# Three first columns of q and k instead of two in fp32, with the expert weights in another buffer

## The chip, the cores and the metric

The kernel runs on one core of a Trainium2 chip. The metric is the device time of one execution in microseconds (us). Most runs of one kernel here lie within half a microsecond of its median, and single ones are a microsecond longer, so differences below that need many runs. All runs quoted are in the fast state; "a slow run" below means only one of the longer runs within it. Engines: PE is TensorE (PEld its weight loads), DVE VectorE, ACT ScalarE, POOL GpSimd, SP SyncE.

## The reference, cut to what matters

```python
# attention over channels: B, N, C = 4, 6400, 256
qn = q / (norm(q, axis=1) + 1e-06);  kn = k / (norm(k, axis=1) + 1e-06)
a = softmax(kn.transpose(0, 2, 1) @ qn / tau)        # 256 x 256 for each batch
x = (v @ a).reshape(B * N, C)
# two of 8 experts by gate, adapters of rank 16
out = x + sum_e w_e * (x @ A[e]) @ B[e]
```

For each batch all of q and k has to be read before the 256 x 256 matrix is complete; only then can v be used. Inputs and output are fp32 in HBM: 78.91 MB are read and 26.21 MB written.

## The kernel before: the parts that matter

A small planner in Python decides the order of instructions on each engine; at run time each engine keeps that order. q and k of a batch are cut into 50 columns of 128 rows x 256 values and loaded in three pieces, most of them by GpSimd with a cast to bf16 during the DMA. The first piece of batch 0 is special: it is cut into 2 + 15 columns, and the 2 columns come in fp32 from SyncE (q) and ScalarE (k), whose DMAs can be issued at time 0. ScalarE then casts them.

```python
PARTS = {(0, 0): ((0, 2), (2, 15)), ...}
# ... cut ...
def load_consts():
    first = W["first"].rearrange("p c d -> p (c d)")         # the same buffer "y0" as q and k below
    W["A0"] = first[0:P // 4, 4 * C:8 * C].rearrange("p (e g r) -> p e g r", e=E, r=R)
    nc.sync.dma_start(W["A0"], moe_A.rearrange("e (p g) r -> p e g r", g=8))
    W["B0"] = first[:, 8 * C:9 * C]
    nc.scalar.dma_start(W["B0"], moe_B.rearrange("e r d -> (e r) d"))
    W["wg0"] = first[0:P // 4, 9 * C:9 * C + 4 * CC * E].rearrange(...)
    nc.scalar.dma_start(W["wg0"], moe_w_gate.rearrange(...))
# ... cut ...
def do_load(s, what, b, i, c, n):
    # ... cut ...
        if (b, c) == (0, 0):
            if "first" not in W:
                W["first"] = sbuf.tile([P, PC, C], FP32, tag="y0", name="y")
            lo = "qk".index(what) * n
            W[what] = W["first"][:, lo:lo + n, :]
            early.append((nc.sync if what == "q" else nc.scalar).dma_start(W[what], src[b, :, 0:n, :]))
            return
    nc.gpsimd.dma_start(t[:, c - c0:c - c0 + n, :], src[b, :, c:c + n, :])
# ... cut ...
def do_cast(s, what):
    nc.scalar.copy(held["qk", (what, 0, 0), ""][:, 0:PARTS[0, 0][0][1], :], W[what])
```

`y0` and `y1` are output buffers, free until the first outputs are written after 60 us.

## Time and profile before

| | before |
|---|---|
| time, median of 3 runs | 255.24 us (255.18 to 255.48) |
| the profiled run | 256.1 us, span 254.3 us |
| TensorE busy | 85% |
| GpSimd's DMA queue, share of the 16 DMA engines | 74.9% |

The page's slices of the kernel before (40 equal slices of 6.4 us; a digit is the busy share in tenths; GB/s counts bytes written):

```profile
PE   1064993799999998999979999979999979999970
...
DMA  9999999999999999999999999999999999999994
GB/s 201 210 216 209 212 222 210 211 219 216 213 218 211 304 290 293 272 217 217 213 215 221 214 215 218 214 209 344 287 273 338 333 328 315 315 421 427 416 411 167
```

Its queue table (queue, packets, MB written, share of the 16 engines' span):

```profile
q0 software_dynamic: 7488, 39.06, 74.9%
q1 hardware_dynamic: 3968, 26.61, 25.7%
q10 hardware_dynamic: 336, 0.40, 0.5%
```

q0 is GpSimd's casting queue: it writes half of what it reads. 39.06 MB in 190 us (74.9% of the span) is 205 GB/s written, so about 410 GB/s read.

TensorE's waits up to 70 us in the kernel before (us in total, times, longest):

```profile
PE acc L571 <- DMA qk<-in_k_dram: 14.0, 3, 9.2
PE acc L571 <- ACT qk L751: 4.8, 1, 4.8
```

The same in the timeline (start, us, instruction, idle time before it and what ended it):

```profile
4.81 1.03 PE L571 MATMUL acc<-qk 128*128 128x256 bf16 x4 [4.81 <-ACT qk L751]
...
15.06 2.32 PE L571 MATMUL acc<-qk 128*128 128x256 bf16 x10 [9.21 <-DMA qk<-in_k_dram]
...
25.35 0.39 PE L571 MATMUL acc<-qk 128*128 128x256 bf16 x2 [3.47 <-DMA qk<-in_k_dram]
```

TensorE uses the two early columns by 5.8 us, then stands still until the 15-column k lands, then again until the 17-column k lands. And the chain of waits of the kernel before (start, us, what):

```profile
4.74 25.52 DMA qk<-in_k_dram
...
30.54 22.25 DMA v<-in_v_dram
```

Two DMA pieces make up 47.8 us of the first 52.8 us of the chain.

### The profile page before, as it was taken

What the parts mean: (1) busy time and instruction counts of PE and PEld (TensorE: products, weight loads), DVE (VectorE), ACT (ScalarE), POOL (GpSimd) and SP (SyncE); (2) the same over time, 40 slices, a digit from 0 to 9 for tenths busy, and PEclk for the clock granted to TensorE, in tenths of its full rate; (3) what the DMA queues carried; (4) which work ended last, traced back from release to release, by engine and by line L of the source; (5) the groups of instructions that cost most, each with busy time, mean ns of one, the idle gap of its engine ahead of it and who ended that gap; (6) DMA issues with size and microseconds to landing.
All of it is one profiled execution on the core that took longest, in us unless ns stands there. A gap on an engine that the chain in (4) does not pass through costs nothing.

```text
span 254.3 us, 6342 instructions
## 1 busy us (share of the span) xinstructions
PE 215.6 (85%) x2641; PEld 192.6 (76%) x2643; DVE 190.2 (75%) x486; ACT 167.2 (66%) x270; POOL 30.0 (12%) x58
## 2 busy tenths in 40 slices
PE   1064993799999998999979999979999979999970
PEld 0043891588999996799879999769999869999860
DVE  0045579779989987898979995689888888888910
ACT  4354447457787666888848768452867969768770
POOL 7000220040020002000030100510000210000000
PEclk9999799799999999999999999999999999999997
DMA  9999999999999999999999999999999999999994
GB/s 201 210 216 209 212 222 210 211 219 216 213 218 211 304 290 293 272 217 217 213 215 221 214 215 218 214 209 344 287 273 338 333 328 315 315 421 427 416 411 167
DMA packets 11820, 66.47 MB, mean 261 GB/s; under 512 B 1424, under 2 KB 2320, under 8 KB 7184
## 3 DMA queue, kind: packets, MB, share of 16 engines
q0 software_dynamic: 7488, 39.06, 74.9%
q1 hardware_dynamic: 3968, 26.61, 25.7%
q10 hardware_dynamic: 336, 0.40, 0.5%
q8 instruction: 20, 0.33, 0.5%
q14 instruction: 8, 0.07, 0.1%
HBM read 78.91 MB, written 26.21 MB: 413 GB/s over the span
## 4 chain that ended last, share of the span: by engine, by line
PE 49%; DMA 39%; ACT 3%; DVE 3%; POOL 2%; issue 1%; ACTq 0%; POOLq 0%
DMA qk<-in_k_dram 22%; PE Y_ps L890 13%; DMA v<-in_v_dram 9%; DMA qk<-in_q_dram 8%; PE acc L571 7%; PE Y_ps L894 6%; PE T_ps L766 6%; PE ZL_ps L788 4%; PE gzT_ps L877 3%; PE acc L580 2%; PE acc L575 2%; PE Z_ps L857 2%; DVE a_bf L740 2%; ACT a_exp L692 1%; PE log_ps L803 1%
## 5 line engine op out<-in xcount | busy, mean ns | idle before, releaser
L571 PE MATMUL acc<-qk 128*128 128x256 bf16 x400 | 71.0, 286 | 21.0 <-DMA qk<-in_k_dram 15.7
L599 DVE TENSOR_TENSOR ssq<-ssq,sq 128x1280 f32<-128x1280 f32 (+1 forms) x27 | 43.4, 1607 | 27.6 <-ACT sq L593 25.6
L890 PE MATMUL Y_ps<-a_bf,vT 128*128 128x256 bf16 x400 | 60.0, 273 | 0.0
L593 ACT ACTIVATE sq<-qk 128x1280 f32<-128x1280 bf16 (+1 forms) x27 | 36.9, 1366 | 26.5 <-DVE ssq L599 19.7
L746 ACT COPY y<-Y_ps 128x512 f32<-128x512 f32 x79 | 45.8, 587 | 12.3 <-PE Y_ps L894 9.8
L571 PEld LDWEIGHTS <-qk 128*128 128x128 bf16 x400 | 33.9, 103 | 25.0 <-DMA qk<-in_k_dram 17.4
L746 ACT COPY vT<-T_ps 128x1024 bf16<-128x1024 bf16 (+1 forms) x44 | 37.0, 871 | 6.7 <-PE T_ps L766 6.5
L890 PEld LDWEIGHTS <-vT 128*128 128x128 bf16 x400 | 37.6, 98 | 3.7
L894 PE MATMUL Y_ps<-ball,gzT 128*128 128x256 bf16 x200 | 38.2, 273 | 0.3 <-DVE gzT L748 0.3
L575 PE MATMUL acc<-qk 128*128 128x128 bf16 x242 | 34.4, 225 | 0.0
L556 POOL DMA_DIRECT2D v<-in_v_dram x20 | 12.2, 611 | 128.4 <-PE T_ps L766 80.8
L766 PE MATMUL T_ps<-ident,v 128*128 128x128 bf16 x400 | 26.9, 219 | 0.4 <-DMA v<-in_v_dram 0.4
L575 PEld LDWEIGHTS <-qk 128*128 128x128 bf16 x242 | 24.5, 101 | 3.6
L766 PEld LDWEIGHTS <-v 128*128 128x128 bf16 x400 | 23.8, 98 | 1.6 <-DMA v<-in_v_dram 1.2
L866 DVE TENSOR_TENSOR gz<-zl,gateg 128x512 bf16<-128x512 f32 (+1 forms) x42 | 23.5, 597 | 0.3
L580 PE MATMUL acc<-qk 128*128 128x128 bf16 x168 | 23.7, 224 | 0.0
L894 PEld LDWEIGHTS <-gzT 128*128 128x128 bf16 x200 | 19.4, 98 | 3.0 <-DVE gzT L748 0.6
L788 PE MATMUL ZL_ps<-waA_sb,vT 128*128 128x136 bf16 x280 | 19.6, 222 | 1.1 <-DVE waA_sb L734 0.9
L877 PE MATMUL gzT_ps<-ident,gz 128*128 128x128 bf16 x200 | 19.7, 219 | 0.3
L593 ACT ACTIVATE ssq<-qk 128x1536 f32<-128x1536 bf16 x8 | 11.9, 1483 | 11.1 <-DMA qk<-in_q_dram 6.2
L748 DVE COPY gzT<-gzT_ps 128x512 bf16<-128x512 bf16 (+1 forms) x39 | 15.0, 390 | 5.5 <-PE gzT_ps L877 4.8
L788 PEld LDWEIGHTS <-vT 128*128 128x128 bf16 x280 | 17.6, 98 | 1.8 <-issue 1.5
(79 smaller groups left out, 272.3 us busy)
## 6 DMA issues: line engine op xcount, KB each, us to landing
out_dram<-y SPq DMA_DIRECT2D x18, 1280.0 KB, 18.2
v<-in_v_dram POOLq DMA_DIRECT2D x20, 640.0 KB, 20.5
qk<-in_q_dram POOLq DMA_DIRECT2D x7, 1088.0 KB, 23.9
qk<-in_k_dram POOLq DMA_DIRECT2D x7, 1088.0 KB, 28.8
qk<-in_q_dram POOLq DMA_DIRECT2D x2, 1024.0 KB, 18.7
qk<-in_k_dram POOLq DMA_DIRECT2D x2, 1024.0 KB, 23.0
out_dram<-y SPq DMA_DIRECT2D x4, 512.0 KB, 7.0
qk<-in_q_dram POOLq DMA_DIRECT2D x2, 512.0 KB, 17.3
```

Of the source, the lines that this page charges most:

```text
L571: nc.tensor.matmul(acc[ic][:, 0:256], kt[:, j, ic * P:(ic + 1) * P], qt[:, j, :], start=c == 0, stop=False, skip_group_check=True)
L575: nc.tensor.matmul(acc[ic][:, 256:384], kt[:, j, ic * P:(ic + 1) * P], kt[:, j, ic * P:(ic + 1) * P], start=False, stop=False, skip_group_ ...
L580: nc.tensor.matmul(acc[ic][:, 384:512], qt[:, j, ic * P:(ic + 1) * P], qt[:, j, ic * P:(ic + 1) * P], start=False, stop=c == NC - 1, skip_ ...
L593: nc.scalar.activation(out[:, 0:n, :], t[:, j:j + n, :], ACT.Square)
L599: nc.vector.tensor_tensor(out=t, in0=t, in1=held["sq", (w, b, g), ""][:, 0:n, :], op=OP.add)
L746: nc.scalar.copy(out, in_)
L766: nc.tensor.matmul(ps[:, ic, j, :], vt[:, c + j, ic * P:(ic + 1) * P], W["ident"], is_transpose=True, start=(ic + j == 0), stop=(ic == CC ...
L788: nc.tensor.matmul(ps[:, j, :], vT[:, ic, c + j, :], st[b]["waA"][:, ic, :], start=(j == 0 and ic == 0), stop=(j == n - 1 and ic == CC - 1 ...
L866: nc.vector.tensor_tensor(out=gz.rearrange("p c (e r) -> p c e r", e=E), in0=z.rearrange("p c (e r) -> p c e r", e=E), in1=held["gate", (b ...
L877: nc.tensor.matmul(ps[:, j, :], gz[:, j, :], W["ident"], is_transpose=True, start=(j == 0), stop=(j == n - 1))
L890: nc.tensor.matmul(ps[:, j, :], vT[:, ic, c + j, :], st[b]["a"][:, ic, :], start=(j == 0 and ic == 0), stop=False, skip_group_check=True)
L894: nc.tensor.matmul(ps[:, j, :], gzT[:, c + j - UNITS[u][0], :], W["B"], start=False, stop=(j == 1), skip_group_check=True)
```

## The change

Its intent: SyncE's and ScalarE's queues start before GpSimd's, so let them bring one column more and let TensorE do it in its idle time. Three fp32 columns of q and k reach over the old place of A, so A, B and the gate weights move to the next buffer. The order of instructions stays the same on every engine.

```diff
+FIRST = 3
@@ load_consts
-        first = W["first"].rearrange("p c d -> p (c d)")
+        first = sbuf.tile([P, PC, C], FP32, tag="y1", name="y").rearrange("p c d -> p (c d)")
@@ do_load
             if (b, c) == (0, 0):
+                n = FIRST
                 if "first" not in W:
@@ do_load
                 return
+        if (what, b, i) in (("q", 0, 0), ("k", 0, 0)):
+            c, n = FIRST, c + n - FIRST
         nc.gpsimd.dma_start(t[:, c - c0:c - c0 + n, :], src[b, :, c:c + n, :])
@@ do_cast
-        nc.scalar.copy(held["qk", (what, 0, 0), ""][:, 0:PARTS[0, 0][0][1], :], W[what])
+        nc.scalar.copy(held["qk", (what, 0, 0), ""][:, 0:FIRST, :], W[what])
```

## The prediction

> What bounds the kernel now. The page's slices show the 16 DMA engines 9 tenths busy or more in 39 of 40, and the queue table says why: the casting GpSimd queue holds 74.9% of the engines' time, SyncE's queue (stores, q's first load) 25.7%. Both cost the same per fp32 byte: 39.06 MB written as bf16 in 190 us is 205 GB/s, so about 410 GB/s read; SyncE's 26.61 MB in 65 us is 407 GB/s. TensorE is second: 85% busy, near 10 tenths from 55 to 245 us. Before that it follows the loads: by the list of waits its accumulation waits 14.0 us for k to land (9.2 of it until 15.05 us, 3.5 until 25.35 us). The chain of waits is one DMA piece from 4.74 to 30.26 us and another (v) from 30.54 to 52.8 us.
>
> What the change does. No engine's order of instructions changes. q's and k's first fp32 loads grow from 256 to 384 KB each; the next GpSimd loads shrink from 15 to 14 columns. HBM bytes read stay equal; 0.13 MB more is written to SBUF. The casts grow from 0.61 us to an estimated 0.85 us each (from this trace's copies, 587 ns for 512 columns, 871 ns for 1024). The weights move to the second output buffer, since three columns reach over their old place; they are consumed by 37 us, and no output is written before 60 us, so this costs nothing.
>
> What lies on the critical path. Not TensorE's third column: it is 2 matmuls, about 0.5 us (4 took 1.03 us), moved from behind 15.05 us into idle time; but afterwards TensorE waits for the 17-column k load until 25.35 us anyway, so only that wait grows. What could count is the DMA: the first GpSimd load is issued at 1.42 us and its first packet appears about 3.6 us; until then only the fp32 loads and weights feed the engines. In narrow windows the engines move nothing from 4.5 to 4.6 us and little until 4.8. From 2 to 5 us they read (written bytes plus the GpSimd bytes once more) an estimated 1.10 MB of the 1.24 that about 410 GB/s would give, a loss near 0.35 us. 256 KB (0.64 us at 407 GB/s) moved to queues that start first can fill part of that hole. I credit 0.1 to 0.3 us, which shifts every later load, since the GpSimd queue hardly runs empty afterwards. The Trainium skill ("DMA: Bandwidth & Descriptors", section "Issuing engines are not separate DMA queues") says that DMAs of all issuers run on the same 16 engines and interleave; the trace agrees (queue shares add to about 1.0). So moving bytes between issuers wins nothing but the hole.
>
> Prediction: 255.0 us, 254.3 to 255.6 for 8 in 10. Faster by over 2%: 1%; within 2%: 98%; slower: 1%.
>
> What would show each step. The first matmul starts near 5.6 to 6.0 us instead of 4.81 (longer load, longer casts), with 6 matmuls instead of 4. The 14-column k lands at 14.7 to 15.0 us (the 15-column one let TensorE start at 15.05), q's at 10.3 to 10.7 us (10.4 before). TensorE's wait before the next k load grows to about 4 us and ends at 25.0 to 25.3 us. The v load that TensorE waits for lands 0.1 to 0.3 us before 52.79. The queue table keeps its sum of shares.
>
> What would make it wrong. The fp32 packets delaying the GpSimd stream more than they fill (0.2 us slower); a shift of tenths that tips a TensorE clock window after 55 us, or the order of stores and loads there, worth up to 0.5 us either way; descriptor generation on GpSimd, not data, setting the pace in the first 5 us: no gain.

## The result, and the profile after

Six runs each on one chip: 255.34 us after (255.29 to 255.96), 255.38 us before (255.18 to 256.68). The ratio is 0.9992, with a 95% interval of 0.9969 to 1.0015. Ratios are the mean time of one kernel's fast runs over that of the other's of the same rounds, so not quite the ratio of the medians quoted.

The slices of the kernel after:

```profile
PE   1173993899999999999989999979999979999970
...
DMA  9999999999999999999999999999999999999994
GB/s 223 211 215 212 212 217 213 213 216 216 218 215 211 318 295 293 259 214 219 209 216 221 217 216 217 210 211 345 284 278 323 331 322 319 316 421 427 427 411 196
```

Its queue table:

```profile
q0 software_dynamic: 7488, 38.93, 74.8%
q1 hardware_dynamic: 3968, 26.74, 26.0%
q10 hardware_dynamic: 336, 0.53, 0.6%
```

0.13 MB left q0, and twice as many fp32 bytes were added to the other two; the sum of the shares is as before.

TensorE's waits up to 70 us after:

```profile
PE acc L575 <- DMA qk<-in_k_dram: 12.4, 3, 7.5
...
PE acc L575 <- ACT qk L755: 5.6, 1, 5.6
```

The timeline after:

```profile
5.56 1.46 PE L575 MATMUL acc<-qk 128*128 128x256 bf16 x6 [5.56 <-ACT qk L755]
...
14.49 1.89 PE L575 MATMUL acc<-qk 128*128 128x256 bf16 x8 [7.47 <-DMA qk<-in_k_dram]
...
24.87 0.61 PE L575 MATMUL acc<-qk 128*128 128x256 bf16 x2 [4.35 <-DMA qk<-in_k_dram]
```

And the chain after:

```profile
4.74 24.96 DMA qk<-in_k_dram
29.98 22.10 DMA v<-in_v_dram
```

Compared line by line, these two traces tell a story of success: k lands 0.57 us earlier, the next k 0.48 us, v at 52.08 instead of 52.79 us, and the span is 0.8 us shorter. But the times of the kernels are equal. The profiled run of before took 256.1 us, that of after 255.31. Either the gain is real and was given back in most runs, or the trace of before shows a slow run. The first experiments decide between these.

### The profile page after: what moved, and what is told of

Its sections match the earlier page's. It is cut to its first block, busy times and chain, and to the rows that moved or that the text cites. A ratio compares the mean times of both kernels' runs of the same rounds, so it can differ in the third digit from the quotient of the medians.

```text
span 253.5 us, 6344 instructions
## 1 busy us (share of the span) xinstructions
PE 215.6 (85%) x2643; PEld 192.3 (76%) x2643; DVE 190.1 (75%) x486; ACT 167.6 (66%) x270; POOL 29.9 (12%) x58
## 4 chain that ended last, share of the span: by engine, by line
PE 49%; DMA 39%; ACT 3%; DVE 3%; POOL 2%; issue 1%; ACTq 0%; POOLq 0%
DMA qk<-in_k_dram 22%; PE Y_ps L894 13%; DMA v<-in_v_dram 9%; DMA qk<-in_q_dram 8%; PE acc L575 7%; PE Y_ps L898 6%; PE T_ps L770 6%; PE ZL_ps L792 4%; PE gzT_ps L881 3%; PE acc L584 2%; PE acc L579 2%; PE Z_ps L861 2%; DVE a_bf L744 2%; ACT a_exp L696 1%; PE log_ps L807 1%
## 5 line engine op out<-in xcount | busy, mean ns | idle before, releaser
L579 PE MATMUL acc<-qk 128*128 128x128 bf16 x242 | 34.0, 223 | 0.0
L584 PE MATMUL acc<-qk 128*128 128x128 bf16 x168 | 23.5, 222 | 0.0
```

The lines of the kernel that those rows point to most:

```text
L579: nc.tensor.matmul(acc[ic][:, 256:384], kt[:, j, ic * P:(ic + 1) * P], kt[:, j, ic * P:(ic + 1) * P], start=False, stop=False, skip_group_ ...
L584: nc.tensor.matmul(acc[ic][:, 384:512], qt[:, j, ic * P:(ic + 1) * P], qt[:, j, ic * P:(ic + 1) * P], start=False, stop=c == NC - 1, skip_ ...
```

## The experiments

Three jobs of four kernels, five rounds each. In each job the kernel before ran 11 times beside them: its median was 255.34 us in the first job, 255.76 in the second, 255.17 in the third. "TensorE resumes" is the start of the matmuls that wait for the second part of k (15.06 us in the trace of before).

### Before and after, once more

No edit.

> The kernel before once more, unchanged. The profiled run of before took 256.1 us, 0.9 us more than its fastest, the profiled run of after only 255.31, so the two traces may differ by more than the change. Theory S (a gain in the load stream that is later given back): TensorE again resumes on the second part of k near 15.05 us and the span is near 254.3 us while the time is near 255.3. Rival V (run-to-run variation: the profiled run of before was a slow one): TensorE resumes at 14.4 to 14.7 us and the span is near 253.5 us, like the trace of after. Ratio to before 1.000 within 0.001 under both.

> The changed kernel once more. Gain as predicted (0.1 to 0.3 us): ratio to before 0.9988 to 0.9996. Rival V (no gain, the engines were never empty): 0.9995 to 1.0005, and the landing of the second part of k (TensorE resumes) anywhere from 14.4 to 15.1 us, as in before.

Measured: before again 255.51 us, ratio 0.9999 (0.9979 to 1.0019). After again 255.82 us, ratio 1.0005 (0.9979 to 1.0030). The timeline of the unchanged kernel in its second trace:

```profile
4.68 1.04 PE L571 MATMUL acc<-qk 128*128 128x256 bf16 x4 [4.68 <-ACT qk L751]
...
14.54 2.31 PE L571 MATMUL acc<-qk 128*128 128x256 bf16 x10 [8.82 <-DMA qk<-in_k_dram]
...
24.88 0.39 PE L571 MATMUL acc<-qk 128*128 128x256 bf16 x2 [3.39 <-DMA qk<-in_k_dram]
```

The same kernel now resumes at 14.54 us, half a microsecond earlier than in its first trace and almost where the changed kernel did. Rival V is right about the traces: most of the difference between the first two was the run, not the change. Its span (253.8 us, against 253.5 expected) only came near. The changed kernel in its second trace resumes at 14.76 us.

### The weights' buffer alone

```diff
-FIRST = 3
+FIRST = 2
```

on the changed kernel, which leaves two columns, with the weights in the other buffer.

> Only the other part of the change: two first columns, as before, with A, B and gate weights in the second output buffer. Both theories expect no effect: ratio 0.9995 to 1.0005, first matmul at 4.8 us. A difference here over 0.2 us would mean that the place of the weights, not the third column, matters.

Measured: 255.36 us, ratio 1.0000 (0.9980 to 1.0020); the first matmul at 4.64 us, TensorE resumes at 14.79 us. As expected, the buffer costs nothing that these runs show. In trace comparisons this kernel counts below as a third one with two columns.

### Four columns, twice

```diff
-FIRST = 3
+FIRST = 4
```

> Four first columns instead of three, otherwise as after: the dose doubled against before. If each column moved fills part of a hole (the prediction), about 0.2 to 0.5 us less than before, ratio 0.998 to 0.9992. If there is no hole (packets laid over each other keep the engines full from 1 us on), ratio 0.9995 to 1.0010, with the first matmul later again, near 6.3 us.

> The kernel with four columns once more. T: lag again 0.2 to 0.5 us, TensorE resumes at 13.6 to 14.2 us, ratio 0.998 to 0.9992. N: lag 0.5 or more, TensorE resumes later than 14.2 us, ratio 0.9995 to 1.0005.

Measured: 255.08 us, ratio 0.9985 (0.9964 to 1.0007), TensorE resumes at 13.76 us; and 255.13 us, ratio 0.9978 (0.9958 to 0.9997), TensorE resumes at 14.61 us. The times fit theory T (the time follows the slowest of the 16 DMA engines; the expectation of the run with five columns, next, has it in full), but the second trace does not. T's measure, called the lag below, is the time from the median end of the last 24 packets of k's second part to the end of the last one. It was 1.03 us here, where T expected 0.2 to 0.5.

### One column and five columns

```diff
-FIRST = 3
+FIRST = 1      # and, in another kernel, 5
```

> Five first columns. New theory T (slowest engine): what counts is not the mean of the 16 DMA engines but the one that lost most time in the first 6 us; its last packet of the first GpSimd k load ends 1.0 to 1.2 us after the median engine's with two columns (three traces), 0.7 to 0.8 with three (two traces), 0.3 with four (one trace), and that lag stays to the end. T expects 0.2 to 0.4 us of lag here and a time 0.2 to 0.5 us below before, ratio 0.998 to 0.999. Rival N (the run with four was a lucky one): lag anywhere from 0.3 to 1.2, ratio 0.9995 to 1.0005. Both: first matmul near 7 us.

> One first column. T: lag of the slowest engine 1.0 to 1.5 us, k's second part lands at 14.5 to 15.2 us, time 0 to 0.4 us above before. N: no trend, ratio 0.9995 to 1.0005. First matmul near 4 us.

Measured with five: 254.93 us, ratio 0.9966 (0.9948 to 0.9985), faster than before beyond the noise. TensorE resumes at 13.88 us; the lag is 0.35 us. With one: 255.93 us, ratio 1.0000 (0.9982 to 1.0019). The timeline with one column:

```profile
3.96 0.61 PE L575 MATMUL acc<-qk 128*128 128x256 bf16 x2 [3.96 <-ACT qk L755]
...
16.18 2.74 PE L575 MATMUL acc<-qk 128*128 128x256 bf16 x12 [11.61 <-DMA qk<-in_k_dram]
```

The second part of k lands more than a microsecond later than in any trace with two columns (lag 1.94 us), yet this profiled run took 255.42 us, no longer than usual. So T's rule, by which a lag stays and sets the time, does not hold for every lag. v landed at 52.88 us in this trace, against 52.79 in the first trace of before, but not because an engine had caught up. Every GpSimd load ends in 16 packets of 4 bytes (832 for the 52 loads), and TensorE resumes 0.3 to 0.4 us after the last of the 16; they are taken here as the load's ends on the 16 engines. By them the slowest end came 1.91 us after the median for k's second part with one column, and still 1.91 us after it for the load that ends at 52.53 us. In the first trace of before this distance grew from 1.08 us to 2.16 us by then. Why so large a lag costs nothing in the time is open.

### A third time three columns, a second time five

No new edits.

> The changed kernel a third time, on the chip of the next three. If the dose is even (about 0.2 us for each column moved, from the runs with four and five columns): ratio 0.9990 to 0.9996. If nothing comes before the fourth column: 0.9997 to 1.0005. The interval of one job is about 0.002 wide, so this alone cannot decide; it counts together with the two earlier ones.

> Five columns again. If the gain is real: ratio 0.9955 to 0.9985, and in the profile the last store packet ends before 252.2 us while TensorE ends near 245.5 us as in all runs. If the first result was luck of the chip: 0.9990 to 1.0010.

Measured: three columns 255.72 us, ratio 1.0013 (0.9994 to 1.0032), TensorE resumes at 14.68 us. Five columns 254.70 us, ratio 0.9983 (0.9969 to 0.9997); the last packet ends at 251.68 us, before 252.2 as expected, but TensorE ends at 244.8 us and not near 245.5. The timeline with five columns:

```profile
7.38 2.31 PE L575 MATMUL acc<-qk 128*128 128x256 bf16 x10 [7.38 <-ACT qk L755]
...
13.92 1.04 PE L575 MATMUL acc<-qk 128*128 128x256 bf16 x4 [4.23 <-DMA qk<-in_k_dram]
...
24.21 0.61 PE L575 MATMUL acc<-qk 128*128 128x256 bf16 x2 [3.56 <-DMA qk<-in_k_dram]
```

Three columns gain nothing that can be seen: the ratios of three jobs are 0.9992, 1.0005 and 1.0013, their plain mean 1.0003. Five columns are faster in both jobs. On one chip, the six runs with five columns took 254.56 to 254.98 us, those with three 254.95 to 255.90. This is the version that beats both kernels, by 0.2% to 0.3%, well below the 2% that would be called faster.

### One unused megabyte more at the head

```diff
         nc.sync.dma_start(W["A0"], moe_A.rearrange("e (p g) r -> p e g r", g=8))
+        extra = sbuf.tile([P, PC, C], FP32, tag="y6", name="y")
+        nc.sync.dma_start(extra[:, 0:8, :], k_v[B - 1, :, 0:8, :])
```

on the kernel before.

> Before, plus one load of 1 MB of fp32 that nothing uses, issued on SyncE behind A. Price of bytes at the head: if a byte read in the first microseconds delays the end one for one, 1.05 MB at about 415 GB/s is +2.5 us, ratio 1.010 (1.008 to 1.012). If there were idle engines (a hole) in the head that it can fill, or slack later, it costs clearly less: under +1.8 us, ratio under 1.007.

Measured: 259.08 us, 3.3 us more, ratio 1.0127 (1.0107 to 1.0148); TensorE resumes at 17.60 us, 2.8 us later than the mean of the three traces with two columns:

```profile
17.60 2.31 PE L573 MATMUL acc<-qk 128*128 128x256 bf16 x10 [11.95 <-DMA qk<-in_k_dram]
```

More than one for one: a delay of the whole load stream in the head is paid in full at the end. By the 4-byte packets, k's second part ends later here on the fastest, the median and the slowest engine alike (by 2.9, 3.5 and 2.9 us against the means of the three two-column traces). That a gain of the third column would have shown as fully is not shown: with one column TensorE resumed 1.4 us later than with two, in one trace, and the time did not change.

### The weights behind the casts, and no weights

First edit, on the kernel with five columns: the three weight loads are all issued on SyncE after the two casts, over the columns that the casts have read (the tile dependency makes them wait). The earlier call of load_consts is dropped.

```diff
-        first = sbuf.tile([P, PC, C], FP32, tag="y1", name="y").rearrange("p c d -> p (c d)")
+        first = W["first"].rearrange("p c d -> p (c d)")
-        W["B0"] = first[:, 8 * C:9 * C]
-        nc.scalar.dma_start(W["B0"], ...)
+        W["B0"] = first[:, 0:C]
+        nc.sync.dma_start(W["B0"], ...)          # gate weights likewise
@@ do_cast
+        casts.append(what)
+        if len(casts) == 2:
+            load_consts()
```

> Five columns, and A, B and gate weights loaded on SyncE only after the two casts, over the columns they have read. In all traces the engines read at only 200 to 350 GB/s while the weights' packets of 256 to 1024 bytes are among theirs (3.5 to 5.5 us). Theory W (small packets leave engines short in the head because nothing large runs beside them): among the large GpSimd packets they cost less, 0.2 to 0.5 us below five columns alone, ratio 0.9945 to 0.996. Rival: the same cost wherever they run, ratio as with five columns, 0.996 to 0.998.

Measured: 255.37 us, ratio 1.0010 (0.9994 to 1.0025): 0.67 us slower than five columns alone on the same chip. Theory W falls, and the rival's number too. (The expectation's "in all traces" is not so for five columns, where the rate stays at 375 GB/s or more from 3.5 to 5.5 us in the mean of two traces.) The timeline:

```profile
13.85 1.04 PE L575 MATMUL acc<-qk 128*128 128x256 bf16 x4 [4.19 <-DMA qk<-in_k_dram]
...
24.86 0.61 PE L575 MATMUL acc<-qk 128*128 128x256 bf16 x2 [5.30 <-DMA qk<-in_k_dram]
```

TensorE resumes at 13.85 us as with five columns (13.92), but the next k comes at 24.86 instead of 24.21 us, 0.65 us later. The weights are 264 KB, which is 0.270 MB (the expectations write 0.264 MB), and at 410 GB/s this is an estimated 0.66 us. Their packets run from 10.94 to 25.99 us in this trace: there they cost about their full price.

That they cost nothing in the head is true, in these traces, only of the slowest engine. By the 4-byte packets, k's second part ends at a median of 12.60 us here, against 13.33 and 13.10 us in the two traces of five columns with the weights in the head; its slowest end is 13.51 us, against 13.52 and 13.54. At the median the removal gained 0.5 to 0.7 us, but TensorE waits for the slowest, which gained nothing.

Second edit, on the kernel before: no weight loads (VectorE fills their place with 0.01). Its output is wrong, which doesn't matter for the time.

```diff
+        nc.vector.memset(first[:, 4 * C:10 * C], 0.01)
-        nc.sync.dma_start(W["A0"], ...)          # B and the gate weights likewise
```

> Before without the loads of A, B and gate weights; VectorE fills their place with a constant, so the result is wrong on purpose. Their 0.264 MB at 415 GB/s would be worth 0.64 us, at the price the 1 MB load showed (3.3 us for 1.05 MB) 0.83 us: ratio 0.9965 to 0.9978. If small packets cost more than their bytes (theory W): 1.0 to 1.5 us, ratio 0.994 to 0.996. If the head has slack: under 0.3 us, ratio over 0.9988.

Measured: 255.60 us, ratio 1.0016 (1.0000 to 1.0033). Not faster at all; the case "the head has slack" came out. TensorE resumes at 14.58 us:

```profile
14.58 2.31 PE L572 MATMUL acc<-qk 128*128 128x256 bf16 x10 [9.43 <-DMA qk<-in_k_dram]
```

The profile's windows without weights (start and end, length, busy time of PE, PEld, DVE, ACT and POOL, granted clock, DMA share, GB/s written):

```profile
2.50:3.00 0.50, 0.00 (x0) 0.00 (x0) 0.50 (x4) 0.17 (x2) 0.43 (x3) 1.00 1.11 275
3.00:3.50 0.50, 0.00 (x0) 0.00 (x0) 0.07 (x1) 0.50 (x3) 0.50 (x2) 1.00 0.85 92
3.50:4.00 0.50, 0.00 (x0) 0.00 (x0) 0.00 (x0) 0.50 (x2) 0.50 (x2) 1.00 0.85 123
4.00:4.50 0.50, 0.38 (x2) 0.28 (x3) 0.00 (x0) 0.06 (x1) 0.50 (x2) 1.00 0.83 154
4.50:5.00 0.50, 0.50 (x4) 0.15 (x1) 0.00 (x0) 0.00 (x0) 0.50 (x2) 1.00 0.98 200
```

Here is a hole at last: with the fp32 columns done by 3 us and no weights to fill in, the engines wait for GpSimd. Its first load is issued at 1.42 us, its first packet starts at 2.92 us, and full rate (200 GB/s written) comes only at 4.5 us. In the kernel before, the weights' packets lie in this hole (2.8 to 4.7 us in its first trace), which hides a part of their price, not all of it. By the 4-byte packets, k's second part ends at a median of 13.01 us without weights, against 13.61, 13.36 and 13.36 us in the three traces with two columns: 0.43 us earlier, of the estimated 0.66. The slowest end, 14.22 us, lies within those with weights (14.69, 14.16 and 14.44). So by the median the hole hid about a third of the price, and on the slowest no clear gain is left; this is one trace. The VectorE fill did not move GpSimd's issues (1.42, 2.08, 3.15, 3.70 us in both kernels). Why this kernel is, if anything, slightly slower than before is open.

## Why the prediction was right, and where its reason was not

The time, 255.34 us, lies in the range, and "within 2%" was right. But the range, 254.3 to 255.6, holds the kernel before (255.24 us) as well: a change that does nothing would have hit it too, so the hit says nothing for the gain that was credited. The parts:

**No effect of TensorE's third column, of the casts and of the buffer: right.** The two casts took 0.83 us each (0.85 estimated). The first matmul came at 5.56 us (5.6 to 6.0 predicted), TensorE used the third column in idle time, and its wait for the next k grew from 3.47 to 4.35 us (about 4 predicted). The run with only the buffer changed gave a ratio of 1.0000.

**The landings: right in direction, not in place.** The second part of k was to land at 14.7 to 15.0 us and the next k to end TensorE's wait at 25.0 to 25.3 us; in the three traces of the changed kernel TensorE resumes at 14.49, 14.76 and 14.68 us, and the next wait ends at 24.87, 25.05 and 24.98 us. Only the second trace lies in both ranges. v landed 0.7 us earlier in the first pair of traces, where 0.1 to 0.3 were predicted. These numbers were counted from one trace of before, which was a slow run.

**"Moving bytes between issuers wins nothing but the hole", and a shift at the head is paid at the end: right for a delay of the whole stream, not shown for a gain.** The Trainium skill ("DMA: Bandwidth & Descriptors", section "Issuing engines are not separate DMA queues") says so of the issuers, and the sum of the queue shares stayed at about 1.01. The megabyte at the head (+3.3 us) and the moved weights (+0.67 us for 0.65 us at the k load) show delays that reach the end. The late k with one column did not reach it, and the earlier median engine without weights did not help it.

**The hole from 4.5 to 4.8 us, and the gain of 0.1 to 0.3 us: the step that failed.** The prediction read it from windows of 0.1 us. This is how two of them look in the kernel before:

```profile
4.40:4.50 0.10, 0.00 (x0) 0.00 (x0) 0.00 (x0) 0.10 (x1) 0.10 (x1) 1.00 2.58 463
4.50:4.60 0.10, 0.00 (x0) 0.00 (x0) 0.00 (x0) 0.10 (x1) 0.10 (x1) 1.00 0.00 0
```

A share of 2.58 is impossible for engines that can be busy only once. The view counts a packet whole where it starts, and a GpSimd packet here takes 0.59 us: six windows. The zero beside 2.58 is not idleness, it is the same packets still running. Laying each packet of the trace over its own duration gives the following (GB/s read in stretches of 0.5 us from the time in the head row, GpSimd's bytes counted twice because it reads fp32; means over the traces with that many columns):

```
columns, traces   1.0  1.5  2.0  2.5  3.0  3.5  4.0  4.5  5.0  5.5  6.0   MB read, 1.0 to 8.5 us
2 (3)              87  172  379  396  356  217  320  382  413  393  390   2.59
3 (3)              89  107  264  398  414  395  322  272  336  381  410   2.52
4 (2)              79  146  325  410  419  409  398  314  290  415  426   2.68
5 (2)              98  185  314  362  398  416  410  413  375  377  414   2.72
2, no weights (1) 124  286  395  244  127  212  297  381  409  386  393   2.46
```

With two columns the engines are occupied from 2.0 us on (shares of 0.98 to 1.12); what they lack is rate. From 2 to 5 us they read 1.03 MB by this table, even less than the 1.10 of the prediction: the shortage was real, but its place was wrong, and so was the step that bytes moved to the other queues fill it. There is a ramp up to 2.5 us, and a dip while the weights' packets, of 256 to 1024 bytes, are among theirs (3.5 to 4.5 us). The Trainium skill ("DMA: Bandwidth & Descriptors", section "Specifications") gives 512 B as the least transfer at line rate; here even with most packets at 512 and 1024 bytes the rate fell to 217 GB/s, though GpSimd's start falls into the same stretch and no run separates the two. Part of what the prediction listed as a risk is in this too: in the run without weights GpSimd's own start, not the data, sets the pace until 4.5 us. The third column does not fill this dip but pushes it back, to 4.0 to 5.5 us, and the ramp is poorer: 0.23 MB by 2.5 us against 0.32. By 8.5 us the three traces with three columns have read 0.07 MB less in the mean than those with two (2.48 to 2.56 against 2.50 to 2.64), an estimated 0.17 us at 410 GB/s; the spreads overlap.

That k nevertheless lands a little earlier goes with another term. A load has landed when the last of the 16 engines is done: the Trainium skill says so ("DMA: Bandwidth & Descriptors", section "Why a DMA increments its semaphore by 16 and not by 1": "only the full 16 means 'all data landed'"), and the traces agree. In the first trace of before, the median of the last 24 packets of the second part of k ends at 13.63 us, the last at 14.69 us, and TensorE resumes at 15.06 us. This lag was 1.05, 0.99 and 1.17 us in the traces with two columns and 0.70, 0.81 and 0.70 us with three. Less lag and a slower stream would nearly cancel; this is argued from three traces of each, and no run changes one without the other. TensorE resumes at 15.06, 14.54 and 14.79 us with two columns, at 14.49, 14.76 and 14.68 us with three, on average 0.15 us earlier, inside the spread of one kernel. So the credited term, 0.1 to 0.3 us, measured 0.15 us at the landing, which these traces cannot tell from nothing, and it is not visible in the time (mean ratio 1.0003, where the prediction's 255.0 over 255.24 is 0.9991). With intervals of about 0.2% either way in each job, a gain of 0.1 us is not excluded.

**Why two traces misled.** In the ten traces of kernels with two to five columns in which nothing else that costs was changed, the time at which TensorE resumes goes with the time of the same run: 13.76 us with 254.59, 13.88 with 254.91, 13.92 with 254.72, 14.49 with 255.31, 14.54 with 255.55, 14.61 with 255.63, 14.68 with 255.88, 14.76 with 255.84, 14.79 with 255.82, 15.06 with 256.1. A straight line through them has a slope of 1.2 and misses none by more than 0.2 us. So most of what differs between runs of one kernel seems to be there by 15 us, and the first pair of traces is explained by that without any effect of the change. This is a correlation, and it does not show how the start reaches the end. It is already looser at v: TensorE starts on the v piece that it waits for at 51.51 us in the run of 255.82 us (weights' buffer alone), but at 52.12 us in the shorter run of 255.31 us (three columns, first trace). The run with one column (16.18 us, 255.42 us) and the one without weights (14.58 us, 255.95 us) do not lie on the line. The clock granted to TensorE does not order the runs: among the 11 runs of before in the first job the shortest (254.79 us) had 0.976 and the longest (256.69 us) 0.974, and the correlation of clock and time is 0.06.

**What stays open.** Why five columns gain 0.4 to 0.9 us where three gain nothing: in their two traces the dip at the weights is shallow (375 GB/s at its lowest) and the lag 0.35 and 0.54 us, but no run parts the two, and four columns have a deep dip (290 GB/s) and nearly the same gain. Which engine lags, and why, can't be told, since these packet records do not name the engine.

## What to carry to other kernels

When a DMA-bound kernel must wait for its slowest queue to start, a part of the other queues' bytes can be hidden in that time: see what already lies there before adding more, and look at the slowest DMA engine and not only at the mean rate, since a load has landed only when that one is done. A profile window shorter than the packets in it shows holes that are not there; take one several packets long, or check that the neighbouring share does not exceed 1. And before explaining a difference of half a microsecond between two traces, take a second trace of the unchanged kernel.

## What the Trainium skill lacked or had wrong

- "DMA: Bandwidth & Descriptors" ("Latency and other measured facts") gives about 1 us to the first byte of a DMA issued from GpSimd. In the run without weights, 1.5 us passed from the issue at 1.42 us to the first packet at 2.92 us, and full rate came 3.1 us after the issue. The page says nothing of this ramp.
- The same page has no figure for how far the engines drift apart at the start. Here the last packet of a load of about 0.9 MB ended 0.3 to 1.2 us after the median of the load's last 24, and up to 1.94 us with one column; TensorE waits for the last.
- No page that was consulted warns that much of the run-to-run spread of a kernel may arise in its first microseconds: TensorE resumed at 14.54, 14.79 and 15.06 us in three traces of kernels with the same loads.
